# An output unit at the head of each projection group, and one more empty slot in segment 4's plan

## The chip, the core and the metric

The kernel runs on one NeuronCore of a Trainium2 chip. The metric is the device time of one execution in microseconds (us). The time before is 244.87 us, the median of four runs (244.29 to 245.58).

## What is computed

Causal attention for 4 batches of 8 heads (768 positions, head size 64), then a two-layer projection over its output. Heads 0, 2 and 6 see the whole causal past; the others ("stream" heads) see the first 4 positions and the last 64.

```python
scores = q @ k.T / sqrt(64)
a = softmax(where(mask[head], scores, -1e9))
x = (a @ v), heads side by side              # 3072 x 512
h = x @ w_in                                 # 3072 x 2048
out = (max(h, 0) + alpha * min(h, 0)) @ w_out  # 3072 x 512
```

## The kernel before, in words

**Attention.** The work goes by segments n = 0 to 15: segment n takes the pair of heads `PAIRS[n % 4]` = (0,1), (2,3), (6,7), (4,5) of batch n // 4. A segment has these pieces:

- `Tq(n)`, `Tk(n)` (L272 to L294, n < 8): six TensorE transposes each of queries and keys; ScalarE and VectorE copy them out of PSUM (L275, L288, L292 to L294). From segment 8 on, DMA transposes do this (L164, L184).
- Scores: `SR(n,hh,m)` (`S_retr`, L315), six parts for a full head, and `SS(n,hh,m)` (`S_stream`, L347), three parts for a stream head. TensorE makes the scores (L333, L360), ScalarE the exp (L341, L367), VectorE multiplies by the mask (L345, L371). Two PSUM banks, sc0 and sc1, are used in turn.
- `AV(n,hh)` (L375): 27 (full) or 13 (stream) small matmuls of the exps with v (L387), then VectorE takes reciprocals (L392) and writes the normalised rows xn (L393).
- `X(n)` (L396): seven TensorE transposes of xn (L400) and one VectorE copy into xT (L402), whose chunk n % 4 it fills.

VectorE also casts loaded data to bf16 (`whole_q`, `whole_k`, `whole_v`, L162, L175, L180, L189); ScalarE does a few of these.

**Projection.** The tokens are cut into eight tiles t, of 512 and 256 tokens in turn. `P1(t,f)` (L420) is a unit of matmuls over four chunks of xT (L431), then neg = relu(-h) on ScalarE (L438) and g = h + (1 - alpha) * neg on VectorE (L441). A tile of 512 tokens has 16 such units, one of 256 has 8, each of these with two blocks. `P2(t,s,quarter)` (L446) is four matmuls of g with w_out (L451); after the fourth quarter ScalarE copies the result out (L456) and a DMA stores it (L459). Both take a PSUM bank by `ff_bank`, which picks the one that an estimated clock says is free first: mm2, m2, mm0, mm1, and in the tail also sc0, sc1, m0, m1.

**Order.** The program is written out in one order, and each engine runs its own instructions in that order. For segments 4 to 15 the attention pieces are laid in a list `pieces` (L591 to L609). An empty piece (`lambda: None`) is a slot in which only projection units can come. Between the pieces a planner (L624 to L640) places projection units: each piece adds to a budget the remaining units divided by the remaining pieces of the group, and a unit goes out when the budget has half of its cost. The list of units comes in three groups (`plan`, L620), which `merge` (L611) mixes evenly out of a P2 list and a P1 list:

- group one, up to X(7): P2 of tile 0 with P1 of tile 1, then two P2 units of tile 1
- group two, from X(7) to X(11): the other P2 of tile 1 with P1 of tile 2, then P2 of tile 2 with P1 of tile 3
- group three, from X(11) to X(15): P2 of tile 3 with P1 of tile 4, then P2 of tile 4 with P1 of tile 5

After X(15) the tail (L641) has the P2 of tile 5 with the P1 of tile 6, the P2 of tile 6 with the P1 of tile 7, and the P2 of tile 7. Where `merge` finds both lists of like length it alternates; with 16 P1 and 6 to 8 P2 the first unit is a P1. X(7), X(11) and X(15) finish the xT chunk that the first P1 of the next group reads with its fourth matmul.

Segment 4 has an order of its own (L501): it ends with the scores of its stream head, an empty slot, `Tk(5)`, an empty slot.

Of the kernel before, what the change touches and what calls it, by code (L numbers as in the profile page):

```python
# [14 lines left out]
def kernel(  # L15
# [51 lines left out]
    def bank(tag):  # L67
        return P[:, BANK[tag], :]
# [36 lines left out]
    def heads(n):  # L105
        return PAIRS[n % 4]
# [151 lines left out]
    def misc_tag():  # L258
        n_misc[0] += 1
        return f"m{n_misc[0] % 2}"  # L260
# [11 lines left out]
    def Tq(n):  # L272
        tr = T_bank(natq.pop(n), "mm0" if n < 4 else misc_tag())
        T = row_tokens(n)
        nc.scalar.copy(qT[n % NK][:, 0:S].rearrange("d (p t) -> d p t", t=T), in_order(tr[:, 0:S], T))  # L275

    def Tk(n):
        tr = T_bank(natk.pop(n), "mm1" if n < 4 else misc_tag())
        for hh, h in enumerate(heads(n)):
            T = row_tokens(n, h)  # L280
            rows = slice(64 * hh, 64 * hh + 64)
            kt = kTs[n % NK][hh][rows, :]
            src = in_order(tr[rows, 0:S], T)
            copy = nc.scalar.copy if n >= 4 and hh == 0 else nc.vector.tensor_copy
            if RETR[h]:
                cuts = [0, -(-256 // T), S // T] if n == 0 else [0, S // T]
                for lo, hi in zip(cuts, cuts[1:]):
                    copy(kt[:, 0:S].rearrange("d (p t) -> d p t", t=T)[:, lo:hi, :], src[:, lo:hi, :])  # L288
                continue
            slots = kt.rearrange("d (j m t) -> d j m t", j=7, t=T)  # L290
            a, z = NSINK // T, 748 // T
            copy(slots[:, 0:6, a:128 // T, :], src[:, a:z, :].rearrange("d (j m) t -> d j m t", j=6))  # L292
            nc.vector.tensor_copy(slots[:, 6, a:24 // T, :], src[:, z:S // T, :])
            nc.vector.tensor_copy(slots[:, :, 0:a, :], src[:, 0:a, :].unsqueeze(1).to_broadcast([64, 7, a, T]))  # L294
# [80 lines left out]
    def AV(n, hh):  # L375
        e, vv = ebuf.pop((n, hh)), vb[n % NV]
        pav = bank(misc_tag())[:, 0:NT * (D + 1)].rearrange("p (i c) -> p i c", c=D + 1)
        for i in range(NT):
            if RETR[heads(n)[hh]]:
                terms = [(RO[j] + QS[i] - QS[j], j) for j in range(min(i, 5) + 1)]  # L380
            elif i == 0:
                terms = [(0, 0)]
            else:
                own = SLOT * i + 4 if i < 6 else 5 * SLOT + 152
                terms = [(SLOT * (i - 1) + 128, i - 1), (own, i)]
            for m, (o, j) in enumerate(terms):
                nc.tensor.matmul(pav[:, i, :], e[:, o:o + 128], vv[:, j, hh, 0:D + 1],  # L387
                                 start=(m == 0), stop=(m == len(terms) - 1))
        if hh == 0:
            xn[n] = work.tile([128, NT, 128], bf16, tag="xn", name="xn")  # L390
        rcp = work.tile([128, NT, 1], fp32, tag=f"rcp{hh}", name="rcp")
        nc.vector.reciprocal(rcp, pav[:, :, D:D + 1])  # L392
        nc.vector.tensor_tensor(xn[n][:, :, 64 * hh:64 * hh + 64], pav[:, :, 0:D],  # L393
                                rcp.to_broadcast([128, NT, D]), op=ALU.mult)

    def X(n):  # L396
        nat = xn.pop(n)
        tr = bank_bf(misc_tag())
        for i in range(NT):
            nc.tensor.transpose(tr[:, QS[i]:QS[i] + 128], nat[:, i, :], ident)  # L400
        o = n // 4 % 2 * S
        nc.vector.tensor_copy(xT[:, n % 4, o:o + S], tr[:, 0:S])  # L402
# [17 lines left out]
    def P1(t, f, cs=range(4), where=""):  # L420

        o, w = TOK[t]
        o %= 2 * S
        tag = half_done.pop((t, f)) if (t, f) in half_done else ff_bank(where)
        psg = bank(tag)
        clock[0] += T_UNIT * len(cs) / 4
        blocks = range(f, f + 512 // w)
        for i, fb in enumerate(blocks):
            for c in cs:
                a = PAIRS[c][0] // 2  # L430
                nc.tensor.matmul(psg[:, w * i:w * (i + 1)], w_in_b[:, a, 128 * fb:128 * (fb + 1)], xT[:, c, o:o + w],  # L431
                                 start=(c == 0), stop=(c == 3))
        if cs[-1] < 3:
            half_done[t, f] = tag
            return
        free_at[tag] = clock[0] + T_P1
        neg = work.tile([128, 512], fp32, tag="neg", name="neg", bufs=3)
        nc.scalar.activation(neg, psg, AF.Relu, scale=-1.0)  # L438
        for i, fb in enumerate(blocks):
            c = slice(w * i, w * (i + 1))  # L440
            nc.vector.scalar_tensor_tensor(g_buf[t % 2][:, fb, 0:w], neg[:, c], oma[:, fb:fb + 1], psg[:, c],  # L441
                                           op0=ALU.mult, op1=ALU.add)
# [31 lines left out]
    def p1_units(t, where=""):  # L474
        return [(1, lambda f=f: P1(t, f, where=where)) for f in range(0, 16, 512 // TOK[t][1])]

    def p2_units(t, order=None, where=""):
        order = order or [(s, u) for s in range(TOK[t][1] // 128) for u in range(4)]
        return [(1, lambda s=s, u=u: P2(t, s, u, where)) for s, u in order]


    def seg_scores(n):
        parts = []
        for hh, h in enumerate(heads(n)):
            fn, m = (S_retr, N_R) if RETR[h] else (S_stream, 3)
            if n < 4:
                m = -(-m // 2)
            parts.append([lambda m=m, hh=hh, fn=fn: fn(n, hh, m) for m in range(m)])
        return parts

    def seg_pieces(n):
        sa, sb = seg_scores(n)

        prev = [lambda: AV(n - 1, 1)] if n > 4 else []
        tail = [lambda: X(n - 1)] if n > 4 else []
        nxt = [lambda: Tq(n + 1), lambda: Tk(n + 1)] if n + 1 < CROSS else []
        seq = sa[:1] + prev + sa[1:3] + tail + sa[3:5] + nxt[:1] + sa[5:] + nxt[1:] + sb[:1]
        seq += [lambda: AV(n, 0)] + sb[1:]
        if n == 4:

            seq = sa + sb[:1] + [lambda: AV(n, 0)] + nxt[:1] + sb[1:] + [lambda: None] + nxt[1:] + [lambda: None]  # L501
        return seq, (2 + len(sa[1:3]) if tail else 0)

    whole_q(0)
# [42 lines left out]
    for n in range(4):  # L547
        sa, sb = seg_scores(n)
        last = [lambda: AV(n - 1, 0), lambda: AV(n - 1, 1), lambda: X(n - 1)] if n else [None] * 3
        nxt = [lambda: Tq(n + 1), lambda: Tk(n + 1)] if n < 3 else [None] * 2  # L550
        if len(sa) == 3:
            seq = [sa[0], last[0], nxt[0], sa[1], last[1], nxt[1], sa[2], sb[0], last[2], sb[1]]
        else:
            seq = [sa[0], last[0], sa[1], last[1]] + sb + [lambda: AV(3, 0), last[2]]
        if n == 0:
            seq = sa[:2] + nxt[:1] + sa[2:] + nxt[1:] + sb
        if n == 0:
            seq += [slopes, factors]
        seq = [x for x in seq if x]
# [32 lines left out]
    for n in range(4, NSEG):  # L592
        seq, x_at = seg_pieces(n)
        for i, piece in enumerate(seq):
            pre = []
            if i in (0, 2, 4):
                fn = (whole_q, whole_k, whole_v)[i // 2]
                pre = [lambda m=m, fn=fn: fn(m) for m, lo, hi in ((n + 1, 5, CROSS), (n + 2, CROSS, NSEG)) if lo <= m < hi]
            if i == 4 and n < NSEG - NF:
                pre.append(lambda n=n: load(n + NF))  # L600
            ready = []
            if x_at and i == x_at - 1 and n % 4 == 0:
                ready = [n // 2 - 2, n // 2 - 1]
            pieces.append((pre, piece, ready))
# [6 lines left out]
    def merge(a, z):  # L611

        keyed = [((i + 0.5) / len(x), n, u) for n, x in enumerate((a, z)) for i, u in enumerate(x)]
        return [u for _, _, u in sorted(keyed, key=lambda k: k[:2])]


    second = [p2_units(t, where="" if t < 6 else "tail") for t in range(8)]

    second[0] = p2_units(0, [(s + i, u) for s in (0, 2) for u in range(4) for i in range(2)])
    hidden = [p1_units(t) for t in range(6)]  # L620
    plan = [merge(second[0], hidden[1]) + second[1][:2],
            merge(second[1][2:], hidden[2]) + merge(second[2], hidden[3]),
            merge(second[3], hidden[4]) + merge(second[4], hidden[5])]
    units, budget = plan.pop(0), 0  # L624
    for i, (pre, piece, ready) in enumerate(pieces):
        for f in pre:
# [10 lines left out]
        while units and budget >= units[0][0] / 2:  # L637
            c, u = units.pop(0)
            budget -= c
            u()  # L640
    for _, u in merge(second[5], p1_units(6, where="tail")) + merge(second[6], p1_units(7, where="tail")) + second[7][:4]:  # L641
        u()
    P2_last(7, 1)
    return nc
# [35 lines left out]
```

## Time and profile before

| | |
|---|---|
| median of four runs | 244.87 us |
| the profiled execution's own time | 244.29 us |
| its span, first to last instruction | 242.3 us |
| granted TensorE clock | 1.000 |
| PE busy, 2059 matmuls | 230.7 us (95%) |
| weight loads (PEld) busy | 145.2 us (60%) |
| VectorE (DVE) busy, 398 instructions | 166.2 us (69%) |
| ScalarE (ACT) busy, 255 instructions | 142.6 us (59%) |
| GpSimd (POOL) busy | 48.5 us (20%) |
| L431 (P1 matmuls) | 96.2 us busy, 512 of them |
| L451 (P2 matmuls) | 92.6 us busy, 368 of them |
| L441 (g, VectorE) | 74.8 us busy, 128 of them |

The costs of the page are busy times of one execution. Since matmuls are pipelined, the recorded time of a matmul is longer than the distance to the next one; for TensorE the distances from start to start tell more. In a timeline row the first number is the start in us from the span's start, the second the time, then engine, line, operation and shapes, and in brackets the engine's idle time before it with what ended it. Segment 4 begins at about 42 us, X(7) is at 83.58, X(11) at 135.99, X(15) at 188.78.

### The profile page before, as it was taken

What the parts mean: (1) busy time and instruction counts of PE and PEld (TensorE: products, weight loads), DVE (VectorE), ACT (ScalarE), POOL (GpSimd) and SP (SyncE); (2) the same over time, 40 slices, a digit from 0 to 9 for tenths busy, and PEclk for the clock granted to TensorE, in tenths of its full rate; (3) what the DMA queues carried; (4) which work ended last, traced back from release to release, by engine and by line L of the source; (5) the groups of instructions that cost most, each with busy time, mean ns of one, the idle gap of its engine ahead of it and who ended that gap; (6) DMA issues with size and microseconds to landing.
All of it is one profiled execution on the core that took longest, in us unless ns stands there. A gap on an engine that the chain in (4) does not pass through costs nothing.

```text
span 242.3 us, 5348 instructions
## 1 busy us (share of the span) xinstructions
PE 230.7 (95%) x2059; PEld 145.2 (60%) x2059; DVE 166.2 (69%) x398; ACT 142.6 (59%) x255; POOL 48.5 (20%) x98
## 2 busy tenths in 40 slices
PE   6799899799899999999999999999999999999994
PEld 6688645466576555556667555556666544465553
DVE  7797888867989968887686768785665466542410
ACT  5888287769866566764655567765554344523220
POOL 5568900721030300202011102100000000000000
PEclk9999999999999999999999999999999999999999
DMA  7999999999998999989979911401111101012112
GB/s 213 289 237 172 248 198 202 244 271 249 253 208 169 252 174 230 212 192 222 220 139 199 212 31 32 119 3 43 46 43 47 43 0 43 3 47 83 46 45 87
DMA packets 85377, 34.95 MB, mean 144 GB/s; under 512 B 72536, under 2 KB 83560, under 8 KB 85352
## 3 DMA queue, kind: packets, MB, share of 16 engines
q1 hardware_dynamic: 79368, 25.36, 51.4%
q0 software_dynamic: 5664, 8.91, 16.0%
q10 hardware_dynamic: 320, 0.34, 0.6%
q8 instruction: 16, 0.26, 0.5%
q14 instruction: 9, 0.07, 0.1%
HBM read 27.46 MB, written 6.29 MB: 139 GB/s over the span
## 4 chain that ended last, share of the span: by engine, by line
PE 75%; DVE 9%; ACT 5%; SPq 4%; DMA 3%; issue 2%; POOL 0%; ACTq 0%; DVEq 0%; POOLq 0%
PE P L431 32%; PE P L451 27%; PE P L387 5%; PE P L333 4%; DMA vf<-in_v_dram 3%; SPq L139 3%; PE P L360 2%; ACT eR L341 2%; PE P L265 2%; PE P L468 1%; DVE g L441 1%; ACT eS L367 1%; DVE vb L189 1%; PE P L400 1%; ACT neg L438 1%
## 5 line engine op out<-in xcount | busy, mean ns | idle before, releaser
L441 DVE SCALAR_TENSOR_TENSOR g<-neg,oma,P 128x512 bf16<-128x512 f32 (+1 forms) x128 | 74.8, 611 | 48.3 <-ACT neg L438 46.6
L431 PE MATMUL P<-xT,w_in_b 128*128 128x512 bf16 (+1 forms) x512 | 96.2, 326 | 1.2 <-DVE xT L402 1.2
L451 PE MATMUL P<-w_out_b,g 128*128 128x512 bf16 x368 | 92.6, 379 | 0.0
L438 ACT ACTIVATE neg<-P 128x512 f32<-128x512 f32 x96 | 57.2, 598 | 53.3 <-PE P L431 49.9
L431 PEld LDWEIGHTS <-w_in_b 128*128 128x128 bf16 x512 | 48.3, 98 | 28.9
L451 PEld LDWEIGHTS <-g 128*128 128x128 bf16 x368 | 33.7, 98 | 28.6 <-issue 0.5
L341 ACT ACTIVATE eR<-P 128x455 bf16<-128x455 f32 (+3 forms) x63 | 37.3, 604 | 13.5 <-PE P L333 11.5
L367 ACT ACTIVATE eS<-P 128x384 bf16<-128x384 f32 (+1 forms) x55 | 28.0, 520 | 10.7 <-PE P L360 10.1
L459 POOL DMA_DIRECT2D out_dram<-ot x18 | 10.4, 576 | 99.9 <-ACT ot L456 99.8
L333 PE MATMUL P<-qT,kT 128*128 128x454 bf16 (+10 forms) x132 | 24.0, 269 | 1.1 <-DVE kT L288 0.5
L360 PE MATMUL P<-qT,kT 128*128 128x192 bf16 (+2 forms) x140 | 20.1, 234 | 0.8 <-ACT eR L341 0.6
L393 DVE TENSOR_TENSOR xn<-P,rcp 128x448 bf16<-128x448 f32 x32 | 20.0, 625 | 1.1
L371 DVE TENSOR_TENSOR eS<-eS,ms 128x384 bf16<-128x384 bf16 (+1 forms) x47 | 16.6, 361 | 6.0 <-ACT eS L367 5.6
L456 ACT COPY ot<-P 128x512 f32<-128x512 f32 x23 | 13.5, 587 | 9.8 <-PE P L451 9.7
L333 PEld LDWEIGHTS <-kT 128*128 128x128 bf16 x132 | 11.3, 97 | 11.2 <-issue 2.4
L360 PEld LDWEIGHTS <-kT 128*128 128x128 bf16 x140 | 13.0, 98 | 8.2 <-issue 0.3
L345 DVE TENSOR_TENSOR eR<-eR,mr 128x128 bf16<-128x128 bf16 (+4 forms) x54 | 12.5, 252 | 4.5 <-ACT eR L341 4.4
L387 PE MATMUL P<-vb,eR 128*128 128x65 bf16 x324 | 11.9, 192 | 1.3 <-DVE eR L345 1.3
L387 PEld LDWEIGHTS <-eR 128*128 128x128 bf16 x324 | 11.3, 97 | 2.8 <-DVE eR L345 1.4
L387 PEld LDWEIGHTS <-eS 128*128 128x128 bf16 x260 | 10.6, 97 | 3.6 <-DVE eS L371 0.6
L387 PE MATMUL P<-vb,eS 128*128 128x65 bf16 x260 | 12.0, 193 | 0.7 <-DVE eS L371 0.5
L400 PE MATMUL P<-ident,xn 128*128 128x128 bf16 x112 | 8.9, 219 | 1.4 <-DVE xn L393 1.4
(81 smaller groups left out, 157.5 us busy)
## 6 DMA issues: line engine op xcount, KB each, us to landing
qf<-in_q_dram SPq DMA_DIRECT2D x16, 384.0 KB
vf<-in_v_dram SPq DMA_DIRECT2D x32, 192.0 KB
kf<-in_k_dram SPq DMA_DIRECT2D x31, 192.0 KB
out_dram<-ot POOLq DMA_DIRECT2D x18, 256.0 KB, 3.1
w_in_b<-in_moe_w_in_dram POOLq DMA_DIRECT2D x4, 512.0 KB, 7.3
w_out_b<-in_moe_w_out_dram POOLq DMA_DIRECT2D x4, 512.0 KB, 17.2
out_dram<-ot SPq DMA_DIRECT2D x5, 256.0 KB
vf<-in_v_dram SPq DMA_DIRECT2D x20, 6.0 KB
```

The lines of the kernel that those rows point to most:

```text
L333: nc.tensor.matmul(sc[:, x, a - lo:z - lo], kt[:, 128 * j:128 * (j + 1)], qt[:, c:c + z - a], start=True, stop=not masked)
L341: nc.scalar.activation(e[:, lo:hi].rearrange("p (x c) -> p x c", x=len(parts)), sc[:, 0:len(parts), 0:(hi - lo) // len(parts)], AF.Exp, sc ...
L360: nc.tensor.matmul(sc[:, x, o:o + w], kt[:, 128 * j:128 * (j + 1)], qt[:, 124 * j:124 * j + w], start=True, stop=not on_pe)
L367: nc.scalar.activation(slots, sc[:, 0:len(thirds), 0:384].rearrange("p x (s c) -> p x s c", c=192), AF.Exp, scale=scale)
L371: nc.vector.tensor_tensor(slots, slots, factor, op=ALU.mult)
L387: nc.tensor.matmul(pav[:, i, :], e[:, o:o + 128], vv[:, j, hh, 0:D + 1], start=(m == 0), stop=(m == len(terms) - 1))
L393: nc.vector.tensor_tensor(xn[n][:, :, 64 * hh:64 * hh + 64], pav[:, :, 0:D], rcp.to_broadcast([128, NT, D]), op=ALU.mult)
L431: nc.tensor.matmul(psg[:, w * i:w * (i + 1)], w_in_b[:, a, 128 * fb:128 * (fb + 1)], xT[:, c, o:o + w], start=(c == 0), stop=(c == 3))
L438: nc.scalar.activation(neg, psg, AF.Relu, scale=-1.0)
L441: nc.vector.scalar_tensor_tensor(g_buf[t % 2][:, fb, 0:w], neg[:, c], oma[:, fb:fb + 1], psg[:, c], op0=ALU.mult, op1=ALU.add)
L451: nc.tensor.matmul(bank(po[t, s]), g_buf[t % 2][:, f, 128 * s:128 * (s + 1)], w_out_b[:, f, :], start=(f == 0), stop=(f == 15))
L456: nc.scalar.copy(ot, bank(po.pop((t, s))))
```

## The change

Three of the edits put one P2 unit in front of a merged list: `second[t][:k] + merge(second[t][k:], ...)`. It is done for group two, group three and the tail; group one is as it was. The fourth adds one more empty slot behind `Tk(5)` in segment 4. No instruction is added or taken away.

```diff
         if n == 4:
-            seq = sa + sb[:1] + [lambda: AV(n, 0)] + nxt[:1] + sb[1:] + [lambda: None] + nxt[1:] + [lambda: None]
+            seq = sa + sb[:1] + [lambda: AV(n, 0)] + nxt[:1] + sb[1:] + [lambda: None] + nxt[1:] + [lambda: None] * 2
...
     plan = [merge(second[0], hidden[1]) + second[1][:2],
-            merge(second[1][2:], hidden[2]) + merge(second[2], hidden[3]),
-            merge(second[3], hidden[4]) + merge(second[4], hidden[5])]
+            second[1][2:3] + merge(second[1][3:], hidden[2]) + merge(second[2], hidden[3]),
+            second[3][:1] + merge(second[3][1:], hidden[4]) + merge(second[4], hidden[5])]
...
-    for _, u in merge(second[5], p1_units(6, where="tail")) + merge(second[6], p1_units(7, where="tail")) + second[7][:4]:
+    for _, u in second[5][:1] + merge(second[5][1:], p1_units(6, where="tail")) + merge(second[6], p1_units(7, where="tail")) + second[7][:4]:
         u()
```

In the order that comes out of it, a P2 unit follows directly on X(7), on X(11), and (behind the last unit of group three) on X(15). In group one, seven units change places with a neighbouring piece: P2(0,0,3) now comes before SR(5,0,4), P1(1,6) before SR(5,0,5), P2(0,1,3) before SS(5,1,0), P2(0,2,0) before SS(5,1,1), P2(0,3,1) before Tk(7), P2(0,2,2) before AV(6,0) and P1(1,12) before SS(6,1,2). The orders on SP and POOL stay the same. Later units take other banks of the same set.

## The prediction

> **What bounds the kernel now.** I read four views in turn: the page's row of slices (which engine, when), the busy time by stretch, the waits of the projection stretch, and the timeline at the places where the diff acts.
>
> ```profile
> PE   6799899799899999999999999999999999999994
> DVE  7797888867989968887686768785665466542410
> ```
>
> A slice is 6.06 us. TensorE is near full from the third slice to the last but one, with dips up to slice 11; VectorE is full in slices 11 to 15, 60 to 91 us. The stretches sharpen this. The columns are length, then busy time of PE, weight loads, DVE, ACT and POOL, the granted clock and the DMA share:
>
> ```profile
> 56.50:66.70 10.20, 9.29 (x107) 6.41 (x104) 8.72 (x28) 8.51 (x17) 1.47 (x3) 1.00 1.10 255
> 66.70:83.60 16.90, 16.41 (x181) 11.31 (x182) 15.96 (x46) 10.52 (x21) 4.15 (x8) 1.00 1.07 208
> 83.60:135.00 51.40, 50.94 (x455) 31.54 (x455) 39.48 (x96) 31.62 (x61) 6.53 (x15) 1.00 1.12 201
> 190.00:235.00 45.00, 44.79 (x240) 23.34 (x239) 19.94 (x35) 18.44 (x31) 1.63 (x3) 1.00 0.11 42
> ```
>
> From 66.7 to 83.6 VectorE is busy 15.96 of 16.90 us: there TensorE waits for it. From 83.6 on TensorE has hardly a gap, at a clock of 1.00, so a gap closed there should reach the end. In the waits of 85 to 192 us TensorE itself has one entry, three times:
>
> ```profile
> PE P L431 <- DVE xT L402: 1.2, 3, 0.5
> ```
>
> These are the three group boundaries, behind X(7), X(11) and X(15). The timeline of TensorE there (start, time, line; in brackets the idle time before it):
>
> ```profile
> 83.98 0.81 PE L431 MATMUL P<-xT,w_in_b 128*128 128x512 bf16 x3
> 85.25 0.38 PE L431 MATMUL P<-xT,w_in_b 128*128 128x512 bf16 x1 [0.46 <-DVE xT L402]
> 85.46 0.36 PE L333 MATMUL P<-qT,kT 128*128 128x45 bf16 x2
> ```
>
> ```profile
> 136.38 0.81 PE L431 MATMUL P<-xT,w_in_b 128*128 128x512 bf16 x3
> 137.74 0.38 PE L431 MATMUL P<-xT,w_in_b 128*128 128x512 bf16 x1 [0.55 <-DVE xT L402]
> 137.96 0.36 PE L333 MATMUL P<-qT,kT 128*128 128x45 bf16 x2
> ```
>
> ```profile
> 190.03 0.81 PE L431 MATMUL P<-xT,w_in_b 128*128 128x512 bf16 x3
> 191.05 0.38 PE L431 MATMUL P<-xT,w_in_b 128*128 128x512 bf16 x1 [0.21 <-DVE xT L402]
> 191.27 1.02 PE L451 MATMUL P<-w_out_b,g 128*128 128x512 bf16 x4
> ```
>
> Each time the first P1 of a group runs three of its matmuls and stops before the fourth, which reads the part of xT that X's copy is still writing. The bracket understates it, since a matmul's recorded end includes its way through the pipe. I count from start to start: a unit of four 512-column matmuls takes 0.86 us (L451 starts at 189.17, the next unit at 190.03).
>
> **Part 1: an output unit first.** The next work should start at 83.98 + 0.86 = 84.84 and starts at 85.46; at 137.24, and starts at 137.96; at 190.89, and starts at 191.27. The stalls are 0.62, 0.72 and 0.38, together 1.72 us. The change puts one P2 unit, which reads older g alone, in front of that P1. At the first two boundaries a scores piece (0.20) stands between them too. The fourth matmul then comes 0.86 to 1.06 us later, more than each stall, so the waits are covered: -1.72 us. If the cover fails at one of them, that stall comes back in full.
>
> Two rules of the Trainium skill speak against it. "Perfetto Trace Analysis", section Identifying the Most-Contended Engine, says that matmul occupancy is a bad measure and that weight-load busy share should be used; that is 60% on the page, so TensorE would have room, the gaps would be absorbed, and part 1 would be worth 0. But between 190 and 235 us units start every 0.86 us without waits while the other engines are half idle: there is no room, and I keep 1.72. "TensorE: Matmul & The Clock Gate", section Back-to-back issue gap, gives about 131 ns for a sustained 512-column matmul, so an estimate of 0.52 us for a unit: that still covers the third stall, but at the second 0.52 + 0.20 only equals the 0.72. The trace has 216 ns (0.86 / 4), and decides.
>
> The other units of groups two and three and of the tail keep their number; a P2 and a P1 change places. AV and X still have as many units in front of them as before. The bank choices change, so I summed TensorE's work between a bank's release and its next use: shortest 3.2 us before, 3.4 after, against under 2 us from a P1's end to the end of its g (74.22 to 75.97 for P1(1,12)). No wait there: 0. The instruction orders on SP and POOL do not change, so no load or store is moved past another.
>
> **Part 2: the second empty slot.** It issues nothing. It stands behind the unit P2(0,0,2), so between Tk(5)'s transposes and the next scores nothing new is placed, and the wait there (0.51 us at 53.42 for the key copy) stays. What it does is to let the planner of group one give seven units to other neighbours, all in the stretch where VectorE and ScalarE are full. I re-timed this stretch by hand, with the durations of the rows and the new order on each engine:
> - Up to 56.8 us nothing differs. Then P2(0,0,3), P1(1,6), P2(0,1,3) and P2(0,2,0) each come before a scores piece, not behind it. The last exp of segment 5's first head (SR(5,0,5)) falls behind neg(1,6) (59.23 becomes 60.0), and its masks behind the two g instructions (end 60.20 becomes 61.29): AV(5,0), at 60.63 as before, reaches them after some 0.4 and waits 0.15.
> - The exp of SS(5,1,1), now behind P2(0,2,0), moves from 61.80 to 62.80. ScalarE was full, so natq's cast, the next exp and neg(1,8) all shift by 0.37, and with them g(1,8) and xn on VectorE. X(5), which waits for that xn already, goes from 66.72 to 67.09: +0.37. A wait of 0.57 of SR(6,0,0) for its bank lies in front of X(5)'s wait and is hidden by it.
> - The dear one is at AV(6,1):
>
> ```profile
> 73.18 1.03 PE L431 MATMUL P<-xT,w_in_b 128*128 128x256 bf16 x8
> 74.22 0.28 PE L387 MATMUL P<-vb,eS 128*128 128x65 bf16 x4
> 74.97 0.59 PE L387 MATMUL P<-vb,eS 128*128 128x65 bf16 x9 [0.47 <-DVE eS L371]
> 75.41 1.03 PE L451 MATMUL P<-w_out_b,g 128*128 128x512 bf16 x4
> ```
>
> ```profile
> 74.57 0.62 DVE L371 TENSOR_TENSOR eS<-eS,ms 128x384 bf16<-128x384 bf16 x2
> 75.10 0.87 DVE L441 SCALAR_TENSOR_TENSOR g<-neg,oma,P 128x256 bf16<-128x256 f32 x2
> ```
>
> Today both masks (74.57) precede g(1,12) (75.10). After the change P1(1,12) comes before SS(6,1,2). From 67.09 TensorE needs 6.27 us to reach that P1 (three P2 and a P1 3.45, AV 0.81, X 0.40, Tq and Tk 0.68, scores 0.93, from start to start), so 73.4, and its results stand at 74.42. Then neg (to 75.05), SS2's exp (to 75.45), the g pair first (to 76.11), the mask (to 76.38). AV(6,1) gets that far by 74.8 and must stop until 76.4; the next unit starts at 76.6, not 75.41: +1.2, of which 0.37 was carried in.
> - Afterwards TensorE leads and VectorE follows; older small waits (AV(7,1), X(7)) take back about 0.15. X(7) comes at 84.6 instead of 83.58: **+1.03 us**.
>
> Bounds for part 2: 0 or a little below, if these waits are taken in by the other waits of this stretch (2.5 us of them before X(7): 0.93 at X(5), 0.8 at AV(6,1), and small ones); upwards, the same kind of wait (masks behind g) cost AV(4,0) 1.27 us at 48.21. I take 1.03, since the path is continuous in the rows.
>
> **The sum.** -1.72 + 1.03 = -0.69 us. The profiled execution took 244.29 us for a span of 242.3 (2.0 us lie around it), so it would take 243.6. It is the quickest of the four runs; on their median of 244.87 this gives **244.2 us**, -0.28%. Measuring tells about 0.5% from no change, that is 243.65 to 246.09.
>
> **Rivals.**
> - Absorbed slot (27%): group one's waits swallow the reordering, only part 1 counts: 244.87 - 1.72 = 243.15. For it: 2.5 us of waits are there, and SP's loads do not move. Against: VectorE has under 1 us of idle time in 16.9.
> - First boundary lost (10%): VectorE is still behind after X(7), and the 0.62 is waited out at the next AV: 1.03 - 0.72 - 0.38, about -0.1, 244.8. Against: VectorE is busy only 39.48 of the next 51.40 us.
> - Slower (8%): masks queued behind g on VectorE, in 56 to 84 us. If AV(5,0) waits as AV(4,0) did (1.27 in place of 0.15) and the 0.57 bank wait is not hidden, group one costs 1.03 + 1.12 + 0.57 = 2.72, and the end is 1.0 later: 245.9. It decides as soon as group one loses over 1.72.
> - The worked sum (50%), 243.7 to 244.7; the remaining 5% lie anywhere.
>
> **How the numbers follow.** Likeliest is the worked sum, 244.2. Low end: the absorbed slot with run-to-run spread, 243.0; high end: part 2 at 1.7 to 2, 245.2, leaves out most of the slower case. Faster by over 0.5% needs the absorbed slot and a tail of the worked sum: 0.33; slower by over 0.5% the third rival: 0.08; within, 0.59.
>
> **What would show it.** Right: no wait of L431 for xT L402 in the changed profile; AV(6,1) (L387, near 75 us) with a wait of over a microsecond for DVE eS L371, with a g pair before that mask; X(7) about 1 us later than 83.58; after X(7) the same work 0.4 later, after X(11) 0.3 earlier, after X(15) 0.7 earlier. Wrong: X(7) at 83.6 or earlier (the slot is free or a gain), X(7) past 85.3 (the slot outweighs the boundaries), or new TensorE waits between 86 and 190 us.

## The result and the profile after

The changed kernel takes 244.11 us (median of 35 runs) against 244.74 us for the kernel before (56 runs beside it): ratio 0.9972, 95% interval 0.9963 to 0.9981. By the ratio that is 0.7 us less (0.5 to 0.9); the forecast was 244.2, or 0.69 less. The profiled execution took 243.88 us, its span is 241.9 us instead of 242.3.

First the busy time by stretch, in the windows and columns of the prediction:

```profile
66.70:83.60 16.90, 15.08 (x174) 10.88 (x175) 15.31 (x43) 10.28 (x21) 3.94 (x8) 1.00 1.08 203
83.60:135.00 51.40, 51.40 (x459) 31.45 (x456) 40.08 (x99) 31.75 (x62) 6.48 (x15) 1.00 1.10 196
135.00:190.00 55.00, 55.00 (x482) 33.85 (x481) 37.66 (x91) 33.11 (x63) 5.18 (x12) 1.00 0.25 60
190.00:235.00 45.00, 45.00 (x242) 23.51 (x241) 19.89 (x35) 18.44 (x31) 1.63 (x3) 1.00 0.11 42
```

In the kernel before, the row from 135 to 190 us was

```profile
135.00:190.00 55.00, 54.45 (x475) 33.26 (x474) 36.76 (x90) 32.55 (x62) 5.55 (x12) 1.00 0.21 55
```

TensorE is now busy in all of the 151.4 us from 83.6 to 235 (150.18 of them before) and has lost 1.3 us between 66.7 and 83.6 (15.08 for 16.41): a gain behind X(7) and a loss in front of it. Next the timeline of TensorE at the three boundaries, behind X(7), X(11) and X(15):

```profile
85.25 1.03 PE L451 MATMUL P<-w_out_b,g 128*128 128x512 bf16 x4
86.12 0.36 PE L333 MATMUL P<-qT,kT 128*128 128x45 bf16 x2
86.32 1.02 PE L431 MATMUL P<-xT,w_in_b 128*128 128x512 bf16 x4
87.18 0.36 PE L333 MATMUL P<-qT,kT 128*128 128x106 bf16 x2
```

```profile
137.91 0.36 PE L333 MATMUL P<-qT,kT 128*128 128x45 bf16 x2
138.11 1.02 PE L431 MATMUL P<-xT,w_in_b 128*128 128x512 bf16 x4
```

```profile
189.12 1.89 PE L451 MATMUL P<-w_out_b,g 128*128 128x512 bf16 x8
190.84 1.03 PE L431 MATMUL P<-xT,w_in_b 128*128 128x512 bf16 x4
```

The first P1 of each group is one piece of four matmuls, with no bracket between the third and the fourth; the next piece starts 0.86 us after it (86.32 to 87.18). In the waits of 85 to 192 us TensorE has no entry left.

In front of X(7), the place the prediction named, AV(6,1) on TensorE and the masks and g on VectorE:

```profile
73.51 1.04 PE L431 MATMUL P<-xT,w_in_b 128*128 128x256 bf16 x8
74.38 0.50 PE L360 MATMUL P<-qT,kT 128*128 128x192 bf16 x5
74.72 0.28 PE L387 MATMUL P<-vb,eS 128*128 128x65 bf16 x4
75.55 0.30 PE L387 MATMUL P<-vb,eS 128*128 128x65 bf16 x4 [0.54 <-DVE eS L371]
76.59 0.33 PE L387 MATMUL P<-vb,eS 128*128 128x65 bf16 x5 [0.75 <-DVE eS L371]
76.76 1.03 PE L451 MATMUL P<-w_out_b,g 128*128 128x512 bf16 x4
```

```profile
75.14 0.35 DVE L371 TENSOR_TENSOR eS<-eS,ms 128x384 bf16<-128x384 bf16 x1
75.40 0.87 DVE L441 SCALAR_TENSOR_TENSOR g<-neg,oma,P 128x256 bf16<-128x256 f32 x2
76.19 0.35 DVE L371 TENSOR_TENSOR eS<-eS,ms 128x384 bf16<-128x384 bf16 x1
```

AV(6,1) now stops twice. The stop before its fifth matmul was there before (0.47, now 0.54). The one before its ninth is new, and ends with a mask that stood behind the g pair. The next unit starts at 76.76 instead of 75.41.

The distances between the starts of X (the L400 rows) cut the program into stretches. In e1, e7 and e9, which are one and the same program, those behind X(4) repeat to 0.01 us, so they show each edit by itself; what lies in front of X(4) does not repeat. In us:

| kernel | start to X(4) | X(4)-X(5) | X(5)-X(7) | X(7)-X(8) | X(8)-X(11) | X(11)-X(12) | X(12)-X(15) | X(15)-L468 |
|---|---|---|---|---|---|---|---|---|
| before | 56.19 | 10.53 | 16.86 | 14.26 | 38.16 | 15.21 | 37.58 | 46.59 |
| changed | 56.33 | 10.90 | 17.62 | 13.64 | 38.16 | 14.49 | 37.58 | 46.23 |
| output unit first, one slot (e1) | 55.92 | 10.53 | 16.85 | 13.64 | 38.16 | 14.49 | 37.58 | 46.23 |
| same (e7) | 56.70 | 10.53 | 16.86 | 13.64 | 38.16 | 14.49 | 37.58 | 46.23 |
| same (e9) | 56.78 | 10.53 | 16.85 | 13.64 | 38.16 | 14.49 | 37.58 | 46.23 |
| second slot alone (e2) | 56.63 | 10.90 | 17.61 | 14.26 | 38.16 | 15.21 | 37.58 | 46.60 |
| changed, P1(1,12) held (e3) | 56.37 | 10.89 | 16.92 | 13.64 | 38.16 | 14.49 | 37.58 | 46.23 |
| changed, P2(0,2,0) held too (e4) | 56.96 | 10.68 | 16.92 | 13.64 | 38.16 | 14.49 | 37.58 | 46.23 |
| changed, g behind the mask (e5) | 56.87 | 10.89 | 17.17 | 13.64 | 38.16 | 14.49 | 37.58 | 46.23 |
| without the first boundary (e6) | 57.56 | 10.53 | 16.85 | 14.47 | 38.16 | 14.49 | 37.58 | 46.23 |
| e1 + queries of 6 early (e8) | 55.28 | 10.90 | 16.85 | 13.69 | 38.16 | 14.49 | 37.58 | 46.23 |
| same (e10) | 56.26 | 10.52 | 16.85 | 13.64 | 38.16 | 14.49 | 37.58 | 46.23 |
| queries of 6 and 8 early (e11) | 55.21 | 10.52 | 16.97 | 14.26 | 38.16 | 14.49 | 37.58 | 46.23 |

From before to changed: +0.37 and +0.76 up to X(7), then -0.62, -0.72 and -0.36. The sum is -0.57 us, and with the +0.14 in front of X(4) -0.43, the 0.4 by which the two spans differ.

### The profile page after: what moved, and what is told of

It is laid out like the page before. It is cut to its first block, busy times and chain, and to the rows that moved or that the text cites. A ratio compares the mean times of both kernels' runs of the same rounds, so it can differ in the third digit from the quotient of the medians.

```text
span 241.9 us, 5348 instructions
## 1 busy us (share of the span) xinstructions
PE 231.0 (95%) x2059; PEld 145.6 (60%) x2059; DVE 166.1 (69%) x398; ACT 142.6 (59%) x255; POOL 48.2 (20%) x98
## 4 chain that ended last, share of the span: by engine, by line
PE 70%; SPq 11%; DMA 6%; DVE 5%; ACT 4%; issue 1%; POOL 0%; DVEq 0%; ACTq 0%; POOLq 0%
PE P L451 28%; PE P L431 26%; SPq L139 6%; PE P L387 5%; DMA qf<-in_q_dram 4%; PE P L333 4%; SPq L141 3%; PE P L360 3%; ACT eR L341 2%; PE P L400 2%; DMA vf<-in_v_dram 2%; PE P L468 1%; ACT eS L367 1%; SPq L126 1%; PE P L265 1%
## 5 line engine op out<-in xcount | busy, mean ns | idle before, releaser
L459 POOL DMA_DIRECT2D out_dram<-ot x18 | 9.8, 545 | 95.4 <-ACT ot L456 94.3
L371 DVE TENSOR_TENSOR eS<-eS,ms 128x384 bf16<-128x384 bf16 (+1 forms) x47 | 17.9, 385 | 5.0 <-ACT eS L367 4.5
L345 DVE TENSOR_TENSOR eR<-eR,mr 128x128 bf16<-128x128 bf16 (+4 forms) x54 | 11.5, 231 | 6.2 <-ACT eR L341 6.1
L155 POOL COPY natk<-natk 4x192 f32<-4x192 f32 x10 | 4.3, 444 | 34.0 <-DVE natk L180 34.0
```

Of the source, the lines that this page charges most:

```text
L371: nc.vector.tensor_tensor(slots, slots, factor, op=ALU.mult)
```

## The experiments

### The two parts apart (e1, e2)

e1 is the changed kernel with the old slot count; e2 is the kernel before with the new one.

```diff
-            seq = sa + sb[:1] + [lambda: AV(n, 0)] + nxt[:1] + sb[1:] + [lambda: None] + nxt[1:] + [lambda: None] * 2
+            seq = sa + sb[:1] + [lambda: AV(n, 0)] + nxt[:1] + sb[1:] + [lambda: None] + nxt[1:] + [lambda: None]
```

This is e1 against the changed kernel; e2 is the same line the other way, in the kernel before.

> The changed kernel without the second empty slot: only the output units at the head of groups two, three and of the tail. Theory (the boundaries give 1.72, the slot costs about 1.1): 244.74 - 1.72 = 243.0, ratio 0.993, with X(7) at the place of before. Rival (the slot is free, and the boundaries give only the measured 0.7): 244.1, ratio 0.997.

> The kernel before with the second empty slot alone. Theory: +1.1 us, 245.85, ratio 1.0045; X(7) some 1.1 us later, three waits for the xT copy as before. Rival (slot free): 244.7, ratio 1.000.

e1: 242.44 us, ratio 0.9902 (0.9871 to 0.9933). e2: 245.83 us, ratio 1.0046 (1.0031 to 1.0060). The slot alone makes the kernel slower by 0.46%, as the theory had it; the rival of a free slot is out. e1 has the stretches of before up to X(7) and those of the changed kernel behind it, as expected, but its time was lower than its stretches explain (-1.70 of them, 0.9931). A part of the rest lay in front of X(4), 55.92 for 56.19 in the profiled executions, so e1 was run again (e7, e9).

### What in the slot costs (e3, e4, e5)

e3 and e4 let the planner pass over one or two pieces; e5 keeps all orders but VectorE's.

```diff
-    units, budget = plan.pop(0), 0
+    units, budget, HELD = plan.pop(0), 0, (41,)
...
-        while units and budget >= units[0][0] / 2:
+        while units and budget >= units[0][0] / 2 and i not in HELD:
```

Piece 41 is SS(6,1,1); e4 has (41, 26), and piece 26 is AV(5,0).

> The changed kernel, but P1(1,12) is held back by one piece, so that it comes behind SS(6,1,2) again, as in the kernel before; all else stays. Theory (the wait at AV(6,1) is the dear part of the slot): 0.76 faster than the changed kernel, 243.35, ratio 0.9943 to before; X(7) only about 0.36 later than in the kernel before. Rival (the loss of group one is spread over the earlier reorderings and VectorE's lag): within 0.2 of the changed kernel, 244.0, ratio 0.997.

> As the run that holds P1(1,12), and P2(0,2,0) is held by one piece as well, behind SS(5,1,1). Theory: both parts of the slot's cost are gone, 243.0, ratio 0.993, X(5) and X(7) at the places of before, though five of the seven moved units are still moved. Rival (the two are not the cause): no better than 243.35 or 244.0.

e3: 243.40 us, ratio 0.9934 (0.9911 to 0.9957). X(5) to X(7) is 16.92: 0.70 of the 0.76 are back by moving one unit one piece. The rival of a loss spread over all reorderings is out for this stretch.

e4: 243.66 us, ratio 0.9943 (0.9923 to 0.9963), not better than e3 as far as the intervals tell; its stretches are, but less than expected: X(4) to X(5) is 10.68, so 0.22 of the 0.37 are back. The other 0.15 is AV(5,0), which waits for its masks before it reaches the held unit: from its start to the next scores TensorE takes 0.97 us there (61.39 to 62.36), 0.81 in the kernel before, and the scores, exps and casts behind it up to X(5) come the same 0.15 later.

In e5, the g instructions of P1(1,12) are written out one piece later (`late` is emptied behind the next piece):

```diff
-        for i, fb in enumerate(blocks):
-            ... scalar_tensor_tensor(...)
+        late.append(lambda: [... scalar_tensor_tensor(...) for i, fb in enumerate(blocks)])
+        (t, f) == (1, 12) or late.pop()()
```

> The changed kernel with TensorE's and ScalarE's orders untouched; only on VectorE the two g instructions of P1(1,12) come behind the mask of SS(6,1,2) instead of before it. Theory (AV(6,1) waits because the mask is queued behind g on VectorE): the mask can end at 76.0 instead of 76.54, so 0.55 of the 0.76 that this spot costs comes back: from X(5) to X(7) 17.07 us (changed kernel 17.62, before 16.86), 243.6. Rival (the scores come too late on TensorE and ScalarE, VectorE's order does not matter): 17.6, 244.1.

e5: 243.96 us, ratio 0.9951 (0.9932 to 0.9969); X(5) to X(7) 17.17. VectorE, then TensorE, in its timeline:

```profile
76.20 0.36 DVE L371 TENSOR_TENSOR eS<-eS,ms 128x384 bf16<-128x384 bf16 x1 [0.17 <-ACT eS L367]
76.47 0.86 DVE L441 SCALAR_TENSOR_TENSOR g<-neg,oma,P 128x256 bf16<-128x256 f32 x2
```

```profile
76.08 0.29 PE L387 MATMUL P<-vb,eS 128*128 128x65 bf16 x4 [0.53 <-DVE eS L371]
76.61 0.33 PE L387 MATMUL P<-vb,eS 128*128 128x65 bf16 x5 [0.24 <-DVE eS L371]
76.78 1.03 PE L451 MATMUL P<-w_out_b,g 128*128 128x512 bf16 x4
```

With g behind it, the mask waits 0.17 for its exp, and the second stop of AV(6,1) shrinks from 0.75 to 0.24. So 0.45 of the 0.76 was VectorE's queue order (0.55 was expected). The remaining 0.31 is not: SS(6,1,2)'s exp still comes late, behind P1(1,12) on TensorE and its neg on ScalarE, which e5 leaves in place and e3 removes (0.70 back). Theory and rival each had a part, in about the proportion 3 to 2.

### Do the boundaries add up (e6)

```diff
-            second[1][2:3] + merge(second[1][3:], hidden[2]) + merge(second[2], hidden[3]),
+            merge(second[1][2:], hidden[2]) + merge(second[2], hidden[3]),
```

This is against e1.

> One empty slot as before; output units first in group three and in the tail, not in group two. Theory (the boundaries add up, 0.61 + 0.71 + 0.37): X(7) to X(8) 14.25 as before, X(11) to X(12) 14.50, 1.1 us faster than before, 243.7. Rival (the first boundary's gain is given back later): the same time as with all three, 242.4 to 243.0.

e6: 244.09 us, ratio 0.9948 (0.9929 to 0.9966; the theory's 1.1 us are 0.9955). The second and third boundary keep their gains in full, and the first stall is back, at 14.47 even 0.2 larger than before. In this execution the cast of v in front of the xT copy took 0.79 us where it took 0.62 in the kernel before; a GpSimd copy (L155) ran beside it and had started 0.03 us ahead of it (85.48). In the kernel before, the cast started first (84.11, the copy at 84.12); there the cast took its 0.62 and the copy 0.81, against 0.33 in e11, where no cast runs beside it. So the later one of the two was the slower one, in these two profiles. The rival, that the first boundary's gain is given back later, is out: all later stretches are the same with and without it.

### The front of the program (e7 to e11)

e7 and e9 are e1 again.

> The output units first at all three boundaries and one empty slot, a second time, since the first time gave 0.990 where 0.993 was expected. Theory (the other 0.6 us was chance in segment 4, whose length differed by 0.6 between executions of the same order): 0.993, 243.1. Rival (removing the slot gives more than its 1.1): 0.990 again.

> The output units first and one empty slot, a third time, as the base of the next two on the same chip: 0.990 to 0.993 of before, about 243.0; X(4) to X(5) 10.53 us, and up to X(4) anything from 55.9 to 57.3 us.

e7: 243.39 us, ratio 0.9930 (0.9903 to 0.9958). e9: 243.21 us, ratio 0.9935 (0.9911 to 0.9958). Both give the expected 0.993, which lies in e1's interval too, so e1's 0.990 was most likely chance. Up to X(4) the three profiles, with one and the same order, need 55.92, 56.70 and 56.78 us.

Before X(4), ScalarE casts segment 6's queries, and waits for their load (0.42, 1.61 and 1.31 us in e1, e7 and e9). X(4) comes 2.49 us after the start of this cast in the kernel before, in the changed one and in e1, e2, e4, e5, e6, e7 and e9, while the cast itself starts anywhere from 53.43 to 55.07. So the landing of these queries sets X(4) in these profiles. In e1, e7 and e9 it is all that differs: behind X(4) they agree to 0.01 us. e8, e10 and e11 move loads, on top of e1. In e11 segment 8's queries are issued before segment 7's values too, and left out where segment 8's keys and values are loaded. This is the edit of e8 and e10:

```diff
-    for n in range(5, 4 + NF):
-        load(n)
+    for x, n in ((load_q, 5), (load_k, 5), (load_q, 6), (load_v, 5), (load_k, 6), (load_v, 6), (load, 7)):
+        x(n)
```

> As the kernel with the output units first and one empty slot, but the load of segment 6's queries is issued before segment 5's values. Theory (segment 4's end hangs on ScalarE's cast of these queries, which waits for their landing and stands before the first exp of segment 5): up to 1 us faster, 242.1. Rival (TensorE's own waits in segment 4 for masks and key copies set its end): within 0.3 of the kernel without this edit, 243.0.

> Segment 6's queries loaded before segment 5's values, a second time. Theory (ScalarE's cast no longer waits for them, but VectorE's cast of segment 8's queries then waits, which gives 0.37 back): 0.3 to 0.7 faster than the base; X(4) at 55.3 or so, X(4) to X(5) 10.90 again. Rival (chance): within 0.2 of the base.

> As the last, and segment 8's queries are loaded before segment 7's values too. Theory (the 0.37 was this landing alone): X(4) to X(5) 10.53, 0.3 to 0.4 faster than the run with segment 6's queries alone, about 242.2. Rival (the values of segment 7 then come late, or another load does): no faster than that run.

The cast of segment 6's queries on ScalarE, in e7 and then in e8:

```profile
54.20 0.83 ACT L162 CAST natq<-qf 128x768 bf16<-128x768 f32 x1 [1.61 <-DMA qf<-in_q_dram]
```

```profile
52.52 0.83 ACT L162 CAST natq<-qf 128x768 bf16<-128x768 f32 x1
```

The wait of 1.61 us is gone. The times: e8 242.64 us, ratio 0.9899 (0.9877 to 0.9920), against 0.9930 for e7 beside it; e10 242.82, 0.9918 (0.9894 to 0.9943), and e11 242.60, 0.9912 (0.9888 to 0.9935), against 0.9935 for e9 beside them. All three medians are lower than the base's, by 0.75, 0.39 and 0.61 us, but the intervals overlap: a gain of some tenths is likely and not shown. Part of it can be lost again. In e8, which came to X(4) at 55.28, VectorE's cast of segment 8's queries waited 0.64 us for their landing, and X(4) to X(5) grew by 0.37; in e10, at X(4) only at 56.26, it did not: there AV(4,0) had waited 1.27 us for a mask, a wait that e8 and e11 do not have (see the last section).

In e11 that cast is free, but X(7) to X(8) is back at 14.26 and X(5) to X(7) 0.12 longer: the 0.37 is gained, 0.74 is lost behind it. The rival, that another load then comes late, is what the trace shows behind X(7), VectorE first and then TensorE:

```profile
84.28 0.63 DVE L189 CAST vb<-vf 128x896 bf16<-128x896 f32 x1 [0.98 <-DMA vf<-in_v_dram]
```

```profile
85.43 0.38 PE L431 MATMUL P<-xT,w_in_b 128*128 128x512 bf16 x1 [0.46 <-DVE xT L402]
```

The cast of segment 10's values waits 0.98 us for its load, X(7)'s copy into xT stands behind it on VectorE, and the fourth matmul of the first P1 waits again, although a P2 unit stands in front of it. The cover has an end: in e8 the same cast waited 0.40 us and X(7) to X(8) grew by 0.05, in e11 by 0.62. Why this load lands later in e11 was not traced.

## Why the prediction was right, step by step

- **The boundaries, -1.72.** Measured -0.62, -0.72 and -0.36, together -1.70. The cover of one unit held at all three, also at the second, where the estimate from the 131 ns of the Trainium skill ("TensorE: Matmul & The Clock Gate", section Back-to-back issue gap) would have left nothing to spare: a unit takes 0.86 us there too. The weight-load share (60%), which the skill ("Perfetto Trace Analysis", section Identifying the Most-Contended Engine) names next to the share of peak FLOP/s as a measure for TensorE, taken alone, as the prediction read it, would have put this part at 0. The stretches show the 1.70 in full, and so do the runs without the slot (0.9930 and 0.9935).
- **AV(5,0) waits 0.15.** Measured 0.15: it holds TensorE from 60.77 to 61.73, 0.96 for 0.81.
- **X(5) comes 0.37 later.** Measured 0.37. Its make-up was told in part: the prediction names the late exp of SS(5,1,1) alone, and e4 shows 0.22 for P2(0,2,0) in front of these scores and 0.15 for AV(5,0)'s wait. The time it gave that exp, 62.80 for 61.80, is one unit (0.86) and that wait together, so the sum had both.
- **AV(6,1).** The next unit was to start at 76.6 and starts at 76.76, in an execution whose X(4) is 0.14 later. The cause was right in kind; e5 shows that the g pair in front of the mask is 0.45 of it and the late exp 0.31. The sign to look for, one wait of over a microsecond, did not come: there are two, of 0.54 and 0.75, since the mask of SS(6,1,1) is late as well, as it was before.
- **X(7) 1.03 later.** Measured 0.37 + 0.76 = 1.13. The term that was off is the 0.15 that older waits were to take back. The next unit behind AV(6,1) is 1.35 us later in the trace and X(7) is 1.27 later, so 0.08 came back, in front of X(6) (0.93 from the unit before it to X(6) in the kernel before, 0.86 now). VectorE was late along with TensorE: its g(1,14) waited 0.59 for the neg of the late P1, where it had not waited before. From this come the other signs too: with the 0.14 taken off, X(8) is 0.5 later (0.4 was forecast), X(12) 0.2 earlier (0.3) and L468 in the tail 0.6 earlier (0.7).
- **The sum.** The stretches give -0.57 for the -0.69. The many executions give -0.7 with an interval of 0.5 to 0.9, which holds both; that their middle falls on the forecast is luck.
- **The slot does nothing behind Tk(5).** So it was: it only gave units other neighbours, and costs 1.13 us.
- **The rivals.** The absorbed slot is excluded by e2, the lost first boundary by e6. The slower case used AV(4,0)'s wait of 1.27 us as a price, as masks queued behind g. That was misread: the rows show a single mask of 1.48 us there, beside GpSimd's casts (last section). It was a poor price too: in the changed profile this wait is missing and Tq(5) comes 1.1 us earlier (48.52 for 49.63), and still X(4) is at 56.33 for 56.19, since ScalarE then waited 1.4 us for the queries. There the wait lay in front of a later one of another engine, and cost nothing. In e10, where the queries are no longer waited for, the same wait is there and X(4) comes about 1 us later than in e8 and e11 (56.26 for 55.28 and 55.21).

The two edits pull against each other: 1.70 us of gain less 1.13 us. The better kernel is the first edit alone, 242.4 to 243.4 us in three measurements, 0.65 to 0.98% below the kernel before.

## What to carry to other kernels

Count a stall from start to start against the same piece's steady pace, not by the bracket: here the brackets added to 1.2 us and the stalls to 1.7. Cover it with a unit whose inputs are long ready, and the gain arrives in full where that engine has no later wait; how long a delay it covers has a limit, as e11 shows. An edit that only shifts a scheduler's slots is not free where TensorE and VectorE are both near full: look for the eviction work that lands before an exp or a mask that the next accumulation needs; moving one unit by one piece gave 0.70 us here.

## What the runs showed of the hardware

I had not expected how long GpSimd's casts can hold a VectorE instruction. In the changed profile, VectorE and then GpSimd:

```profile
47.38 1.55 DVE L371 TENSOR_TENSOR eS<-eS,ms 128x384 bf16<-128x384 bf16 x1
```

```profile
47.46 0.81 POOL L162 CAST natq<-qf 128x768 bf16<-128x768 f32 x1
48.23 0.50 POOL L175 CAST natm<-kf 128x384 bf16<-128x384 f32 x1
```

A mask that takes 0.36 us elsewhere takes 1.55 and ends 0.2 us after the second cast. In the kernel before it was an L345 mask (46.68 to 48.16, 0.22 elsewhere) beside the same two casts (46.81 to 48.07); that was AV(4,0)'s wait. No run was made to take the casts away, but the thirteen profiles differ in when the casts start. In seven (before, changed, e2, e3, e4, e7, e10) a mask runs at that moment and takes 1.3 to 1.6 us. In the other six the masks are over by then, or within their last 0.08 us, and all take their usual time. e7 is among the seven (1.58 us) and e1 and e9, the same program, are among the six (0.36 us both).

The Trainium skill ("SBUF — State Buffer", section Who interferes with whom) describes this: a VectorE instruction with two inputs in SBUF contends with a GpSimd instruction that reads SBUF, since they share a read port, and the one that comes second is blocked until the other ends. The rows agree that one is blocked, and add that it was held over two casts in a row. They do not show the order: the mask's row starts 0.08 us ahead of the first cast's, and still it is the mask that was held.
